# Last feed-forward product: the odd whole block and the half block by Strassen's seven products, with their sums made in the gate and up stage

## The chip, the cores and the metric

The kernel runs on one core of one Trainium2 chip. The metric is the device time of that core in microseconds (us). The kernel before takes 1022.51 us, the median of 3 runs (1022.26 to 1022.66).

## What is computed

```python
g = sigmoid((x * gate_w).sum(-1))                     # one gate for each token
h_re, h_im = x @ dft_hid_re.T, x @ dft_hid_im.T
a = dft_seq_re @ h_re - dft_seq_im @ h_im             # FNet mixing, real part
b = (gelu(x @ w_gate) * (x @ w_up)) @ w_down          # feed-forward with a gated GELU
out = g * a + (1 - g) * b
```

There are S = 2048 tokens, D = 640 features and F = 1728 hidden features, all fp32. In blocks of 128, F is 13 whole blocks and a half block of 64. "The last feed-forward product" is the one by w_down.

## The kernel before

**Parts and tiles.** An fp32 product is made of three matmuls of fp32r parts (`mm3`, L97 to L101): high by high (L99), high by low (L100), low by high (L101). The high part of an operand is a copy on ACT (`high`, L80), the low part a subtraction on DVE (`low`, L83). Everything lives transposed, features on the 128 partitions and tokens along the free dimension in tiles of T = 512. The tokens are two halves `tp` of two tiles each. Raw data, parts and sums share 46 slots of 4 KB a partition (`slot`); single 128x512 tiles come from a second pool of 14 (`mtile`); the eight PSUM banks of 128x512 are shared too (`bank`). A tile taken from a pool waits until the last reader of the tile that was in it is done.

**Strassen.** Most products go by Strassen's method in its form with seven products and shared sums. The four blocks of the left operand are two blocks of input features by two blocks of output features, those of the right operand two blocks of features by the two tiles of a token half. Weights have the blocks A11, A12, A21, A22 and the sums S1 = A21 + A22, S2 = S1 - A11, S3 = A11 - A21, S4 = A12 - S2. Activations have B11 to B22 and the sums T1 = B12 - B11, T2 = B22 - T1, T3 = B22 - B12, T4, as they are called here up to sign. For five output blocks of 128 features, two pairs go by Strassen and the fifth (`e5`, L) by plain products.

**Order of the work.** Five stages follow one another on PE: (1) the first hidden block and the half block (`first_products`, `first_out`), which go to DRAM as `h0[tp]`: entries 0 and 1 are the whole block for the two token tiles, entries 2 and 3 the half block, stacked twice so that it fills 128 partitions; (2) the gate and up stage, hidden blocks f = 1 to 12; (3) the last feed-forward product; (4) the sequence DFT (`cseq`); (5) the hidden DFT and the mixing of the two branches.

*The gate and up stage* (loop at L1094) runs in an order fixed by hand for PE, ACT, DVE and POOL (`in_order`, L1093): each engine works its instructions off in the order in which they were traced. `gate_up` (L485) makes the products of one block for one token half and the gated GELU; from block 3 on, odd blocks come with products across the two halves (`together`, `together_up`). Its sums of activations are, among others, L535, L539, L546, L556 and L563. Finished blocks go from POOL's queue to DRAM (`keep`, L388: `hA`, and the sums `hT`). What is made ready for later blocks is a list of pieces, `fills`, each with a cost: `fill` (L1070) takes pieces from the front while their summed cost is behind 1.25 times the share of PE's work already issued. Among the pieces are the sums and the parts of the next block's weights (`make_w`: sums at L269 to L288, parts by `split`), last sums of the block before (`todo`), the sums of w_down's pair k (`sum_wd`, L590, loads and stores on SP) and the sums of x across the halves (`sums_across`, loads at L1030 on SP; the one called `xv` has its sums at L1034). Blocks also load kept sums (`load_across`: L1065, on POOL, tiles `xq` and `xu`) and, at step 5, the weights of the block after next (on SP).

*The last product* is a list of 28 turns (`kseq`, L716 to L719). For each token half tp they are (b = 0; k = 0 to 5), (0, leftover), (1, 0), (1, leftover), (1; 1 to 5): with b = 0 the four products that need no activation sums, with b = 1 the three others. k is a pair of hidden blocks; the "leftover" (k = NK = 6) is the odd whole block 0 and the half block. The loop (L1171) traces for turn i, in this order: `load_k(i + 3)` (L722, on SP), `split_k(i + 2)` (L771, the parts on ACT and DVE), `late()` (products with the gate and stores of results that are due, L836 and L837), now and then other work (`load_xn` of an x block for stage 4 at the turns in `XN_AT`, L26; the reductions of x for the gate), and `step_k(i)` (L828): the matmuls and, at the end of a group, the copies out of the banks. ACT and DVE run in traced order.

`products` (L812) is what a pair costs: with b = 0, X, Z and V take two `mm3` per bank pair and L takes four, 30 matmuls in all; with b = 1, X, Q, R and Y take 24. The leftover is not by Strassen in the kernel before: `left` (L848) takes an `mm3` for the whole block and, for the half block, two "narrow" matmuls. The half block's 64 input features leave half of the 128 rows free, and these rows carry the low part of the weights (`mx`), so that two matmuls do what otherwise takes three. With b = 0 it goes into V, Z and L (30 matmuls), with b = 1 into R and Y (20); `split_k` makes A11 - A21 and the like by two subtractions at L782. The leftover turn with b = 1 (turn 8, and 22 for the second half) takes the operands of the one with b = 0 (turn 6, and 20) over as they are.

Of the kernel before, what the change touches and what calls it, by code (L numbers as in the profile page):

```python
# [9 lines left out]
F32 = mybir.dt.float32  # L10
F32R = mybir.dt.float32r
AF = mybir.ActivationFunctionType
ALU = mybir.AluOpType

P = 128
S, D, F = 2048, 640, 1728
T = 512
# [5 lines left out]
NF = F // P  # L23
FR = F - NF * P
NK = (NF - 1) // 2
XN_AT = [1, 5, 18, 24]  # L26
GM_AT = [2, 17]
EORD = [0, 2, 1, 3, 4]
PAIRED = 3
# [6 lines left out]
def kernel(  # L36
# [33 lines left out]
    def slot(dt, shape, name):  # L70
        return pool.tile(shape, dt, tag="s4", name=name, bufs=46)

    def mtile(dt, name):
        return pool.tile([P, T], dt, tag="m", name=name, bufs=14)
# [4 lines left out]
    def high(hi, raw):  # L79
        nc.scalar.activation(hi, raw, AF.Copy)  # L80
# [4 lines left out]
    def split(hi, lo, raw):  # L85
        high(hi, raw)
        low(hi, lo, raw)
# [38 lines left out]
    wsu, wneg = ([dram.tile([P, 8, P], F32, tag=f"{n}{p}", name=f"{n}{p}") for p in range(ND)] for n in ("wsu", "wneg"))  # L126
    uA, uT = ([[dram.tile([P, 4, T], F32, tag=f"u{n}{j}{p}", name=f"u{n}{j}{p}") for p in range(ND)] for j in range(2)] for n in "AT")
    grd, gmd = ([dram.tile([1, 2 * T], F32, tag=f"{n}{p}", name=f"{n}{p}") for p in range(2)] for n in ("grd", "gmd"))
    wsd = [dram.tile([P, 8, P], F32, tag=f"wsd{k}", name=f"wsd{k}") for k in range(NK)]
    t4d = [dram.tile([P, 2, T], F32, tag=f"t4{p}", name=f"t4{p}") for p in range(2)]  # L130
    acc4 = dram.tile([P, 2, T], F32, tag="acc4", name="acc4")
# [7 lines left out]
    def at(hilo, i):  # L139
        h, l = hilo  # L140
        return h[:, i], l[:, i]
# [448 lines left out]
    def sum_wd(k):  # L590
# [11 lines left out]

        return [(0, load), (84, do), (84, do)]

    def sum_wu(p):


        r = [mtile(F32, f"ur{p}{k}").rearrange("p (b c) -> p b c", c=P) for k in range(2)]
        a21 = wsmall(F32, f"ua{p}")
        for k in range(2):  # L610
            nc.sync.dma_start(r[k], wu[p, :, 4 * k : 4 * k + 4])
        nc.sync.dma_start(a21, wu[p, :, 8:])
        yield
        if p > 1:
            for k, a, b in ((0, 0, 2), (0, 2, 4), (1, 0, 1), (1, 1, 4)):
                if p < 4 or (k, a) not in ((0, 0), (1, 0)):
                    v = r[k][:, a:b]
                    nc.scalar.activation(v, v, AF.Copy, scale=-1.0)
            if p < 4:
                nc.scalar.activation(a21, a21, AF.Copy, scale=-1.0)  # L620
            for k in range(2):
                nc.gpsimd.dma_start(wneg[p][:, 4 * k : 4 * k + 4], r[k])
            yield
        for _, do in sums_left(nc.gpsimd, r[0][:, 0:2], r[0][:, 2:4], r[1][:, 2:4], a21, wsu[p]):
            do()
        yield
# [95 lines left out]
    def load_k(i):  # L722


        tp, b, k = kseq[i]
        n = f"{tp}{b}{k}"
        if k == NK and b:
            return
        r = slot(F32, [P, 8, P], f"kw{n}")
        if k == NK:  # L730
            m = slot(F32, [P, 8, P], f"km{n}")
            nc.sync.dma_start(r[:, :5], wd0)
            for q in range(2):
                nc.sync.dma_start(m[q * FR : (q + 1) * FR, :5], wdr)
            r, src = (r, m), h0[tp]
        elif b:
            nc.sync.dma_start(r[:, 0:2], wd[k, :, 6:8])
            nc.sync.dma_start(r[:, 2:8], wsd[k][:, 0:6])
            src = hT[tp][k]
        else:  # L740
            nc.sync.dma_start(r[:, 0:6], wd[k, :, 0:6])
            nc.sync.dma_start(r[:, 6:8], wsd[k][:, 6:8])
            src = hA[tp][k]
        raw = []
        for q in range(2):
            raw.append(pair(F32, f"kr{n}{q}"))
            nc.sync.dma_start(raw[q], src[:, 2 * q : 2 * q + 2])
        kraw[i] = r, raw
# [22 lines left out]
    def split_k(i):  # L771
        tp, b, k = kseq[i]
        n = f"{tp}{b}{k}"
        if k == NK and b:
            ktile[i] = ktile[("left", tp)]
            return
        r, raw = kraw.pop(i)
        W = {}
        if k == NK:
            r, m = r  # L780
            for v in (r, m):
                tt(v[:, 5:7], v[:, 0:2], v[:, 2:4], op=ALU.subtract)  # L782
            h, l = slot(F32R, [P, 8, P], f"kh{n}"), slot(F32R, [P, 8, P], f"kl{n}")
            split(h[:, :7], l[:, :7], r[:, :7])
            c, a = slot(F32R, [P, 8, P], f"kc{n}"), slot(F32R, [P, 8, P], f"ka{n}")
            high(c[:, :7], m[:, :7])
            high(a[:FR, :7], m[:FR, :7])
            low(c[FR:, :7], a[FR:, :7], m[FR:, :7])
            W = [at((h, l), q) for q in range(7)], [a[:, q] for q in range(7)]
        else:  # L790
            h, l = slot(F32R, [P, 8, P], f"kh{n}"), slot(F32R, [P, 8, P], f"kl{n}")
            split(h, l, r)
            names = ("A22", "S1", "S2", "S3") if b else ("A11", "A12", "e5", "S4")
            W = {name: (at((h, l), 2 * q), at((h, l), 2 * q + 1)) for q, name in enumerate(names)}
        B = []
        for q in range(2):
            v = hl(f"kb{n}{q}")
            split(*v, raw[q])
            B += [at(v, 0), at(v, 1)]
        ktile[i] = W, B  # L800
        if k == NK:
            ktile["left", tp] = W, B

    kb = {"alone": False}
    after = []
# [22 lines left out]
    def step_k(i):  # L828
# [14 lines left out]
                kb[name] = [bank(f"k{name}{n}{q}") for q in range(2)]  # L843
        X, Z, V, L, Q, R, Y = (kb.get(name) for name in "XZVLQRY")
        if k == NK:
            (f0, mx), first = W, False

            def left(ps, w, t):  # L848
                mm3(ps, f0[w], B[t], False, False)
                for v in B[2 + t]:  # L850
                    nc.tensor.matmul(ps, mx[w], v, start=False, stop=True, skip_group_check=True)

            if b:
                for q in range(2):
                    left(R[q], 2 + q, 1)
                for q in range(2):
                    left(Y[q], 2 + q, 0)
            else:
                for q in range(2):
                    left(V[q], q, 0)  # L860
                for q in range(2):
                    left(Z[q], 5 + q, 1)
                for t in range(2):
                    left(L[t], 4, t)
        else:
            products(kb, b, W, B, fst)
        if not lst:
# [225 lines left out]
    with in_order(PE, ACT, DVE, POOL):  # L1093
        for f in range(1, NF):  # L1094
# [24 lines left out]
            if kind == 1 and f > PAIRED:  # L1119
                (_, first), z1, (_, second), z2 = load_z(2)  # L1120
                first()
                k = len(fills) // 2
                more = list(fills)
                fills.clear()
                fills.extend([*more[:k], z1, (0, second), *more[k:], z2, *work])
            elif f in ZE_AT:
                (_, first), z1 = load_z(1)
                first()
                fills.insert(5, z1)
            if f == NF - 1:  # L1130
                load_k(0)
                fills.extend(split_pieces(0))
                gates(0)
                nc.scalar.activation(table, table, AF.Gelu_apprx_tanh)
# [447 lines left out]
```

## Time and profile before

| quantity | value |
|---|---|
| time, median of 3 runs | 1022.51 us (1022.26 to 1022.66) |
| span of the profiled execution | 1020.7 us |
| matmuls (PE) | 1016.5 us busy, 4491 instructions |
| weight loads (PEld) | 841.3 us, 4491 |
| VectorE (DVE) | 811.4 us, 1143 |
| ScalarE (ACT) | 481.3 us, 631 |
| GpSimd (POOL) | 166.9 us, 295 |
| DMA | 259.19 MB, 254 GB/s on average |

The span runs from the first to the last instruction of one profiled execution; the timed runs hold 1.8 us more around it. DVE is VectorE, ACT ScalarE, SP and POOL the engines that issue DMAs. Rows of the timeline give start, duration, engine, line, operation, and "output<-inputs" by the program's names, in which numbers of buffers are left out in some views; a bracket gives the idle time ahead and what ended it. Rows of the DMA list give output<-input, queue, operation, count, KB of each and the median from issue to landing. Rows of stretches give, for A:B us, the length, then the busy time (and count) of PE, PEld, DVE, ACT and POOL, the granted clock of TensorE, the busy share of the DMA engines and GB/s.

### The profile page before, as it was taken

What the parts mean: (1) busy time and instruction counts of PE and PEld (TensorE: products, weight loads), DVE (VectorE), ACT (ScalarE), POOL (GpSimd) and SP (SyncE); (2) the same over time, 40 slices, a digit from 0 to 9 for tenths busy, and PEclk for the clock granted to TensorE, in tenths of its full rate; (3) what the DMA queues carried; (4) which work ended last, traced back from release to release, by engine and by line L of the source; (5) the groups of instructions that cost most, each with busy time, mean ns of one, the idle gap of its engine ahead of it and who ended that gap; (6) DMA issues with size and microseconds to landing.
All of it is one profiled execution on the core that took longest, in us unless ns stands there. A gap on an engine that the chain in (4) does not pass through costs nothing.

```text
span 1020.7 us, 13172 instructions
## 1 busy us (share of the span) xinstructions
PE 1016.5 (100%) x4491; PEld 841.3 (82%) x4491; DVE 811.4 (79%) x1143; ACT 481.3 (47%) x631; POOL 166.9 (16%) x295
## 2 busy tenths in 40 slices
PE   9999999999999999999999999999999999999998
PEld 7888888888888888888888888888888888888887
DVE  6976878777677979886898975898588859797796
ACT  5544534353535566465455343444344444454440
POOL 0122242323231200100011022102210200021112
PEclk9999999999999999999999999999999999999999
DMA  7445587968698988968766788658866867987856
GB/s 270 168 152 212 181 270 251 295 216 292 201 309 297 406 319 305 358 229 303 269 233 190 249 265 310 215 193 293 302 207 209 298 248 274 324 318 221 264 150 95
DMA packets 92628, 259.19 MB, mean 254 GB/s; under 512 B 12112, under 2 KB 26576, under 8 KB 92560
## 3 DMA queue, kind: packets, MB, share of 16 engines
q1 hardware_dynamic: 66640, 176.98, 50.6%
q0 software_dynamic: 25776, 81.30, 24.6%
q8 instruction: 35, 0.57, 0.2%
q14 instruction: 33, 0.27, 0.1%
q10 hardware_dynamic: 144, 0.07, 0.0%
HBM read 186.19 MB, written 68.17 MB: 249 GB/s over the span
## 4 chain that ended last, share of the span: by engine, by line
PE 100%; DVE 0%; issue 0%
PE pX L101 7%; PE pX L99 7%; PE pX L100 7%; PE pZ L101 5%; PE pZ L99 5%; PE pZ L100 5%; PE pL L101 3%; PE pL L99 3%; PE pL L100 3%; PE pV L101 2%; PE pV L99 2%; PE pV L100 2%; PE pY L101 1%; PE pR L101 1%; PE pQ L101 1%; PE pY L100 1%
## 5 line engine op out<-in xcount | busy, mean ns | idle before, releaser
L80 ACT ACTIVATE ch<-csa 128x1024 fp32r<-128x1024 f32 x32 | 34.0, 1063 | 89.7 <-DVE csa L703 66.9
L83 DVE TENSOR_TENSOR cl<-cra,ch 128x1024 fp32r<-128x1024 f32 x32 | 39.1, 1223 | 21.7 <-ACT ch L80 21.5
L80 ACT ACTIVATE ch<-cra 128x1024 fp32r<-128x1024 f32 x32 | 33.9, 1059 | 46.2 <-PE pL L100 16.9
L83 DVE TENSOR_TENSOR cl<-crb,ch 128x1024 fp32r<-128x1024 f32 x32 | 39.1, 1222 | 17.3 <-ACT ch L80 17.3
L100 PE MATMUL pL<-cl,xah 128*128 128x512 f32 x128 | 49.8, 389 | 0.0
L101 PE MATMUL pL<-ch,xal 128*128 128x512 f32 x128 | 49.8, 389 | 0.0
L99 PE MATMUL pL<-ch,xah 128*128 128x512 f32 x128 | 49.3, 389 | 0.0
L388 POOL DMA_DIRECT2D hA<-s x48 | 26.1, 544 | 133.6 <-DVE s L546 113.9
L80 ACT ACTIVATE ch<-crb 128x1024 fp32r<-128x1024 f32 x32 | 33.8, 1055 | 27.5 <-DVE cl L83 11.0
L83 DVE TENSOR_TENSOR cl<-csb,ch 128x1024 fp32r<-128x1024 f32 x32 | 39.2, 1224 | 4.4 <-ACT ch L80 2.3
L83 DVE TENSOR_TENSOR cl<-csa,ch 128x1024 fp32r<-128x1024 f32 x32 | 39.1, 1223 | 3.8 <-PE pR L100 1.7
L83 DVE TENSOR_TENSOR kl<-kw,kh 128x1024 fp32r<-128x1024 f32 (+1 forms) x26 | 31.5, 1213 | 11.1 <-ACT kh L80 11.0
L80 ACT ACTIVATE ch<-csb 128x1024 fp32r<-128x1024 f32 x32 | 34.0, 1062 | 12.3 <-PE pR L101 4.5
L540 ACT ACTIVATE s<-s 128x512 f32<-128x512 f32 x24 | 15.2, 634 | 47.0 <-DVE s L539 47.0
L80 ACT ACTIVATE kh<-kw 128x1024 fp32r<-128x1024 f32 (+1 forms) x26 | 27.1, 1042 | 11.2 <-PE kY L101 3.3
L1243 POOL DMA_DIRECT2D uA<-c x8 | 4.3, 541 | 169.6 <-DVE c L1331 169.3
L837 POOL DMA_DIRECT2D out<-ks x12 | 6.5, 542 | 155.1 <-DVE ks L836 154.5
L145 ACT ACTIVATE s<-pX 128x512 f32<-128x512 f32 x40 | 23.3, 595 | 14.7 <-PE pX L101 14.4
L388 POOL DMA_DIRECT2D hT<-s x48 | 26.0, 541 | 24.2 <-DVE s L563 9.3
L535 DVE TENSOR_TENSOR s<-s,pX 128x512 f32<-128x512 f32 x24 | 16.4, 685 | 15.4 <-PE pX L101 15.4
L100 PEld LDWEIGHTS pL<-cl,xah 128*128 128x128 f32 x128 | 24.0, 188 | 5.0
L101 PEld LDWEIGHTS pL<-ch,xal 128*128 128x128 f32 x128 | 24.0, 188 | 5.0
(3602 smaller groups left out, 3462.0 us busy)
## 6 DMA issues: line engine op xcount, KB each, us to landing
cra<-in_ct SPq DMA_DIRECT2D x64, 512.0 KB, 4.0
crb<-in_ct SPq DMA_DIRECT2D x64, 512.0 KB, 4.9
hA<-s POOLq DMA_DIRECT2D x48, 256.0 KB, 3.8
hT<-s POOLq DMA_DIRECT2D x48, 256.0 KB, 5.5
kr<-hA SPq DMA_DIRECT2D x24, 512.0 KB, 7.4
kr<-hT SPq DMA_DIRECT2D x24, 512.0 KB, 6.9
ux<-uA SPq DMA_DIRECT2D x24, 512.0 KB, 6.3
ux<-uT SPq DMA_DIRECT2D x16, 512.0 KB, 6.3
```

The costliest lines, as they stand in the source:

```text
L80: nc.scalar.activation(hi, raw, AF.Copy)
L83: nc.vector.tensor_tensor(lo, raw, hi.bitcast(F32), op=ALU.subtract)
L99: nc.tensor.matmul(ps, lh, rh, start=first, stop=False, skip_group_check=True)
L100: nc.tensor.matmul(ps, lh, rl, start=False, stop=False, skip_group_check=True)
L101: nc.tensor.matmul(ps, ll, rh, start=False, stop=last, skip_group_check=True)
L145: nc.scalar.activation(m, src, AF.Copy)
L388: nc.gpsimd.dma_start(to[:, i], src)
L535: tt(s5, s5, X, op=ALU.add)
L540: nc.scalar.activation(s2, s2, AF.Gelu_apprx_tanh)
L837: nc.gpsimd.dma_start(acc4[:, t] if tp and e == 4 else out[2 * tp + t, e], src)
L1243: nc.gpsimd.dma_start(to[:, i], src)
```

## The change

The leftover is taken as one more pair of hidden blocks for Strassen: the whole block 0 and the half block. Where the half block stands for A21, A22, B21 or B22, the missing 64 rows count as zero.

- New sums are made in the gate and up stage and kept in DRAM: `wsl` for the weights, `hL[tp]` for the activations. `LEFT_AT` says in which block: 2 (`sum_h0` for tp 0), 4 (`sum_left`, the weights), 6 (`sum_h0_narrow` for tp 0), 8 and 10 (the same two for tp 1). They have their loads and stores on SP and stand in the middle of the block's `fills`.
- The leftover turn with b = 0 now goes into X as well (A11), and takes narrow matmuls alone for V (A12) and Z (S4); L stays as it was. The turn with b = 1 goes by S1, S3 and S2 into R, Q and X, and by narrow matmuls into Y. It loads activations of its own from `hL`, and takes over the weights alone.
- The subtractions in `split_k` go.
- The second x block for stage 4 is traced at turn 7, no longer at turn 5 (`XN_AT`).

```diff
--- before.py
+++ after.py
@@ -23,7 +23,7 @@
 NF = F // P
 FR = F - NF * P
 NK = (NF - 1) // 2
-XN_AT = [1, 5, 18, 24]
+XN_AT = [1, 7, 18, 24]
 GM_AT = [2, 17]
 EORD = [0, 2, 1, 3, 4]
 PAIRED = 3
@@ -126,6 +126,8 @@
     wsu, wneg = ([dram.tile([P, 8, P], F32, tag=f"{n}{p}", name=f"{n}{p}") for p in range(ND)] for n in ("wsu", "wneg"))
     uA, uT = ([[dram.tile([P, 4, T], F32, tag=f"u{n}{j}{p}", name=f"u{n}{j}{p}") for p in range(ND)] for j in range(2)] for n in "AT")
     grd, gmd = ([dram.tile([1, 2 * T], F32, tag=f"{n}{p}", name=f"{n}{p}") for p in range(2)] for n in ("grd", "gmd"))
+    wsl = dram.tile([P, 8, P], F32, tag="wsl", name="wsl")
+    hL = [dram.tile([P, 4, T], F32, tag=f"hL{p}", name=f"hL{p}") for p in range(2)]
     wsd = [dram.tile([P, 8, P], F32, tag=f"wsd{k}", name=f"wsd{k}") for k in range(NK)]
     t4d = [dram.tile([P, 2, T], F32, tag=f"t4{p}", name=f"t4{p}") for p in range(2)]
     acc4 = dram.tile([P, 2, T], F32, tag="acc4", name="acc4")
@@ -602,6 +604,78 @@
 
         return [(0, load), (84, do), (84, do)]
 
+    def chunks(name):
+        return mtile(F32, name).rearrange("p (b c) -> p b c", c=P)
+    def sum_left():
+        w, m, d = chunks("lw"), chunks("lm"), chunks("ld")
+        nc.sync.dma_start(w, wd0[:, :4])
+        for q in range(2):
+            rows = slice(q * FR, (q + 1) * FR)
+            nc.sync.dma_start(m[rows], wdr[:, :4])
+            nc.sync.dma_start(d[rows], wd0[:FR, :4])
+        a11, a21, a22 = w[:, 0:2], w[:, 2:4], m[:, 2:4]
+        own = {}
+        def first():
+            s = own["s"] = chunks("ls")
+            tt(s[:, 0:2], a21, a11, op=ALU.subtract)
+            tt(a21[:FR], a21[:FR], a22[:FR], op=ALU.add)
+            tt(m[:, 0:2], m[:, 0:2], a22, op=ALU.subtract)
+        def second():
+            s = own["s"]
+            tt(a11, a11, a21, op=ALU.subtract)
+            tt(d[:, 0:2], d[:, 0:2], d[:, 2:4], op=ALU.subtract)
+            tt(s[:, 2:4], m[:, 0:2], d[:, 0:2], op=ALU.add)
+            nc.sync.dma_start(wsl[:, 0:4], w)
+            nc.sync.dma_start(wsl[:, 4:8], s)
+        return [(100, first), (100, second)]
+    def sum_h0(tp):
+        f1, f2, b22 = (mtile(F32, f"lf{tp}{k}") for k in range(3))
+        for v, k in ((f1, 0), (f2, 1), (b22, 3)):
+            nc.sync.dma_start(v, h0[tp][:, k])
+        def first():
+            tt(f1, f2, f1, op=ALU.subtract)
+            for k in (0, 2):
+                rows = slice(FR if k else 0, P)
+                nc.sync.dma_start(hL[tp][rows, k], f1[rows])
+            tt(f2[:FR], f2[:FR], b22[:FR], op=ALU.subtract)
+            nc.sync.dma_start(hL[tp][:, 3], f2)
+            tt(b22[:FR], f1[:FR], b22[:FR], op=ALU.subtract)
+            nc.sync.dma_start(hL[tp][:FR, 2], b22[:FR])
+        return [(183, first)]
+    def sum_h0_narrow(tp):
+        d1, d2, b21, b22 = (mtile(F32, f"lg{tp}{k}") for k in range(4))
+        for v, k in ((d1, 0), (d2, 1)):
+            for q in range(2):
+                nc.sync.dma_start(v[q * FR : (q + 1) * FR], h0[tp][:FR, k])
+        for v, k in ((b21, 2), (b22, 3)):
+            nc.sync.dma_start(v, h0[tp][:, k])
+        def first():
+            tt(d2, d2, d1, op=ALU.subtract)
+            tt(b21, b21, b22, op=ALU.subtract)
+        def second():
+            tt(b21, b21, d2, op=ALU.add)
+            nc.sync.dma_start(hL[tp][:, 1], b21)
+        return [(122, first), (61, second)]
+    LEFT_AT = {2: partial(sum_h0, 0), 4: sum_left, 6: partial(sum_h0_narrow, 0), 8: partial(sum_h0, 1), 10: partial(sum_h0_narrow, 1)}
     def sum_wu(p):
 
 
@@ -724,14 +798,19 @@
 
         tp, b, k = kseq[i]
         n = f"{tp}{b}{k}"
+        r = None
+        if not (k == NK and b):
+            r = slot(F32, [P, 8, P], f"kw{n}")
         if k == NK and b:
-            return
-        r = slot(F32, [P, 8, P], f"kw{n}")
-        if k == NK:
+            src = hL[tp]
+        elif k == NK:
             m = slot(F32, [P, 8, P], f"km{n}")
-            nc.sync.dma_start(r[:, :5], wd0)
+            nc.sync.dma_start(r[:, 0:2], wd0[:, 0:2])
+            nc.sync.dma_start(r[:, 2:8], wsl[:, 0:6])
             for q in range(2):
                 nc.sync.dma_start(m[q * FR : (q + 1) * FR, :5], wdr)
+            nc.sync.dma_start(m[:, 5:7], wsl[:, 6:8])
+            nc.sync.dma_start(m[:, 7], wd0[:, 4])
             r, src = (r, m), h0[tp]
         elif b:
             nc.sync.dma_start(r[:, 0:2], wd[k, :, 6:8])
@@ -771,22 +850,22 @@
     def split_k(i):
         tp, b, k = kseq[i]
         n = f"{tp}{b}{k}"
+        r, raw = kraw.pop(i)
         if k == NK and b:
-            ktile[i] = ktile[("left", tp)]
-            return
-        r, raw = kraw.pop(i)
-        W = {}
-        if k == NK:
+            W = ktile.pop(("left", tp))
+        elif k == NK:
             r, m = r
-            for v in (r, m):
-                tt(v[:, 5:7], v[:, 0:2], v[:, 2:4], op=ALU.subtract)
-            h, l = slot(F32R, [P, 8, P], f"kh{n}"), slot(F32R, [P, 8, P], f"kl{n}")
-            split(h[:, :7], l[:, :7], r[:, :7])
             c, a = slot(F32R, [P, 8, P], f"kc{n}"), slot(F32R, [P, 8, P], f"ka{n}")
-            high(c[:, :7], m[:, :7])
+            high(c, m)
             high(a[:FR, :7], m[:FR, :7])
             low(c[FR:, :7], a[FR:, :7], m[FR:, :7])
-            W = [at((h, l), q) for q in range(7)], [a[:, q] for q in range(7)]
+            low(c[:, 7], a[:, 7], m[:, 7])
+            h, l = slot(F32R, [P, 8, P], f"kh{n}"), slot(F32R, [P, 8, P], f"kl{n}")
+            split(h, l, r)
+            W = {name: (at((h, l), 2 * q), at((h, l), 2 * q + 1)) for q, name in enumerate(("A11", "S2", "S1", "S3"))}
+            mx = {"A12": (a[:, 0], a[:, 1]), "A22": (a[:, 2], a[:, 3]), "e5": a[:, 4], "S4": (a[:, 5], a[:, 6])}
+            W = W, (c[:, 7], a[:, 7]), mx
+            ktile["left", tp] = W
         else:
             h, l = slot(F32R, [P, 8, P], f"kh{n}"), slot(F32R, [P, 8, P], f"kl{n}")
             split(h, l, r)
@@ -798,8 +877,6 @@
             split(*v, raw[q])
             B += [at(v, 0), at(v, 1)]
         ktile[i] = W, B
-        if k == NK:
-            ktile["left", tp] = W, B
 
     kb = {"alone": False}
     after = []
@@ -843,25 +920,28 @@
                 kb[name] = [bank(f"k{name}{n}{q}") for q in range(2)]
         X, Z, V, L, Q, R, Y = (kb.get(name) for name in "XZVLQRY")
         if k == NK:
-            (f0, mx), first = W, False
-
-            def left(ps, w, t):
-                mm3(ps, f0[w], B[t], False, False)
-                for v in B[2 + t]:
-                    nc.tensor.matmul(ps, mx[w], v, start=False, stop=True, skip_group_check=True)
+            W, e5, mx = W
+            def narrow(ps, w, v):
+                for part in v:
+                    nc.tensor.matmul(ps, w, part, start=False, stop=True, skip_group_check=True)
 
             if b:
+                for ps, w, t in ((R, "S1", 0), (Q, "S3", 3), (X, "S2", 2)):
+                    for q in range(2):
+                        mm3(ps[q], W[w][q], B[t], False, True)
                 for q in range(2):
-                    left(R[q], 2 + q, 1)
-                for q in range(2):
-                    left(Y[q], 2 + q, 0)
+                    narrow(Y[q], mx["A22"][q], B[1])
             else:
                 for q in range(2):
-                    left(V[q], q, 0)
+                    mm3(X[q], W["A11"][q], B[0], False, True)
                 for q in range(2):
-                    left(Z[q], 5 + q, 1)
+                    narrow(V[q], mx["A12"][q], B[2])
+                for q in range(2):
+                    narrow(Z[q], mx["S4"][q], B[3])
                 for t in range(2):
-                    left(L[t], 4, t)
+                    mm3(L[t], e5, B[t], False, False)
+                    narrow(L[t], mx["e5"], B[2 + t])
         else:
             products(kb, b, W, B, fst)
         if not lst:
@@ -1127,6 +1207,11 @@
                 (_, first), z1 = load_z(1)
                 first()
                 fills.insert(5, z1)
+            if f in LEFT_AT:
+                more = LEFT_AT[f]()
+                k = len(fills) // 2
+                rest = [fills.pop() for _ in range(len(fills) - k)]
+                fills.extend([*more, *reversed(rest)])
             if f == NF - 1:
                 load_k(0)
                 fills.extend(split_pieces(0))
```

## The prediction

> **What bounds the kernel now.** I read the page first, then what TensorE (PE) waited for, then stretches of the span, then the two engines that feed PE around the changed turns.
>
> ```profile
> span 1020.7 us, 13172 instructions
> PE 1016.5 (100%) x4491; PEld 841.3 (82%) x4491; DVE 811.4 (79%) x1143; ACT 481.3 (47%) x631; POOL 166.9 (16%) x295
> PE 100%; DVE 0%; issue 0%
> PE idle L935 <- PEq L1570: 0.8, 1, 0.8
> 340.00:360.00 20.00, 20.00 (x90) 16.57 (x89) 19.43 (x25) 9.96 (x13) 3.25 (x6) 1.00 1.03 400
> 380.00:400.00 20.00, 20.00 (x90) 16.57 (x89) 17.22 (x20) 13.95 (x16) 2.16 (x4) 1.00 0.88 310
> ```
>
> PE is busy for 1016.5 of 1020.7 us, the chain that ended last is PE throughout, and the list of its waits has a single row, 0.8 us ahead of the first matmul. In the last product (third number of the two stretches) PE is busy 20.00 of 20.00 us at a granted clock of 1.00, while DVE is busy 19.43 and 17.22. So time falls only with the number of matmuls, and rises only where a feeder comes too late. The medians of the timed runs (1022.51 us) lie 1.8 us above this span; I carry that 1.8 us over unchanged.
>
> **The matmuls.** The last product's turns show what a matmul costs:
>
> ```profile
> 374.20 0.62 PE L99 MATMUL kV<-kb0060h,kh 128*128 128x512 f32 x2
> 381.00 0.39 PE L99 MATMUL kX<-kb0100h,kh 128*128 128x512 f32 x1
> 386.44 0.39 PE L99 MATMUL kR<-kb0060h,kh 128*128 128x512 f32 x1
> 390.98 0.39 PE L99 MATMUL kX<-kb0110h,kh 128*128 128x512 f32 x1
> 396.42 0.61 PE L99 MATMUL kX<-kb0120h,kh 128*128 128x512 f32 x2
> 398.46 0.39 PE L100 MATMUL kQ<-kb0121l,kh 128*128 128x512 f32 x1
> ```
>
> The leftover turn 6 begins at 374.20, turn 7 at 381.00, leftover turn 8 at 386.44, turn 9 at 390.98, turn 10 at 396.42. Turn 7 has 24 matmuls in 5.44 us: 0.2267 us each. Turn 6 has 30 (three kinds of bank, two each, 3 + 2 matmuls): 6.80 us. Turn 8 has 20: 4.54 us. All are 128x512.
>
> In the changed kernel turn 6 has 6 (X) + 4 (V) + 4 (Z) + 10 (L) = 24 matmuls, 6 fewer, and turn 8 has 6 + 6 + 6 + 4 = 22, 2 more. Net 4 fewer for each half of the tokens, 8 in all: 4491 becomes 4483. 8 x 0.2267 = **1.81 us off**. That is the whole gain: the sums that Strassen needs are paid elsewhere. The Trainium skill (TensorE: Matmul & The Clock Gate, Back-to-back issue gap) gives about 131 ns for a sustained 512-column matmul; by it the gain would be 1.05 us. The trace's spacing is 227 ns, and the trace decides.
>
> **The new sums in the gate and up stage.** Twenty more DVE operations in blocks 2, 4, 6, 8 and 10: three of 128x512 (two with 64 rows) in 2, 6, 8 and 10, six of 128x256 in 4. In the built order they follow the first sums of the next block's weights (L284) and stand ahead of L269 (in block 2, of the low part L83). Rows of the same shapes, and what comes behind them:
>
> ```profile
> 125.97 0.69 DVE L556 TENSOR_TENSOR s<-s,s 128x512 f32<-128x512 f32 x1
> 126.58 0.69 DVE L546 TENSOR_TENSOR s<-s,s 128x512 f32<-128x512 f32 x1
> 132.10 0.42 DVE L274 TENSOR_TENSOR ws5r<-ws5r,wa5r 128x256 f32<-128x256 f32 x1
> DVE wd L83 <- ACT wd L80: 12.1, 5, 3.3
> 83.04 1.23 DVE L83 TENSOR_TENSOR wa3l<-wa3r,wa3h 128x1024 fp32r<-128x1024 f32 x1 [2.68 <-ACT wa3h L80]
> 229.01 0.29 DVE L288 TENSOR_TENSOR wb<-wa9r 128x128 f32<-128x128 f32 x1
> 231.85 0.29 DVE L83 TENSOR_TENSOR wd<-wb,wd 128x128 fp32r<-128x128 f32 x1 [2.56 <-ACT wd L80]
> 233.20 0.68 DVE L535 TENSOR_TENSOR s<-s,pX 128x512 f32<-128x512 f32 x1
> 236.68 0.39 PE L99 MATMUL pX<-x05h,wa 128*128 128x512 f32 x1
> ```
>
> One 128x512 sum follows the other after 0.61 us (125.97 to 126.58): three are 1.8 us. Six of 0.34 to 0.42 us are 2.0 to 2.5 us. Right behind the insertion DVE stands idle already: in block 2 for 2.68 us, in the later ones 2.4 us on average (12.1 us in 5 waits, up to 3.3), waiting for ACT's high part. That idle time takes 1.8 us whole, and of 2.0 to 2.5 us nearly all. I also cost it without the cover: block 8's L535 reads X at 233.20 to 233.88 and PE writes X again at 236.68, so 2.8 us of lead; a full shift of 1.8 or 2.5 us leaves 0.3 to 1.0 us. Cost on PE: **0**.
>
> POOL's queue holds one thing behind these sums: the load of the kept sums (L1065) takes a buffer that L288 reads last.
>
> ```profile
> 275.95 0.28 DVE L288 TENSOR_TENSOR wb<-wa11r 128x128 f32<-128x128 f32 x1
> 278.58 0.56 POOL L1065 DMA_DIRECT2D xq<-xp  x1 [0.41 <-issue]
> xq<-xp POOLq DMA_DIRECT2D x12, 512.0 KB, 5.0
> 286.40 0.39 PE L99 MATMUL pZ11t<-xq,wq11h 128*128 128x512 f32 x1
> 276.00:278.00 2.00, 2.00 (x10) 1.67 (x9) 0.23 (x2) 1.60 (x4) 0.70 (x1) 1.00 0.69 135
> kr<-hA SPq DMA_DIRECT2D x24, 512.0 KB, 7.4
> ```
>
> In block 10 L288 ends at 276.23; plus 1.8 it ends at 278.0, just ahead of the issue at 278.58. The load lands after 5.0 us by the median, at 283.6, 2.8 us ahead of PE. New is SP's store of 256 KB beside it; at the 135 GB/s of that stretch it takes 1.9 us if nothing overlaps. Bounds: 0 from the median, (278.58 + 7.4 + 1.9) - 286.40 = 1.5 us of wait from the slower row of 7.4. I take 0, nearer to the row of the same load.
>
> SP's queue: 41 more transfers, about 10 MB beside 259.19 MB on the page. In block 2 the four stores wait for DVE's sums, and the loads of the t4 sums stand behind them.
>
> ```profile
> 72.63 5.46 SPq L1030 DMA_DIRECT2D xv<-t  x4
> 80.08 0.29 DVE L284 TENSOR_TENSOR wq3r<-wa3r,wq3r 128x128 f32<-128x128 f32 x1
> 96.32 0.69 DVE L1034 TENSOR_TENSOR xvt<-xv,xv 128x512 f32<-128x512 f32 x1
> xr<-in_xt SPq DMA_DIRECT2D x11, 256.0 KB, 4.8
> ```
>
> The sums end at about 80.3 + 1.8 = 82.1; two of the four loads also wait for buffers that those stores read, so they go out by about 85 and land, at 4.8 us like other 256 KB loads, at about 90. DVE wants them at 96.32: 6 us to spare. Cost 0.
>
> **The last product's own feeders.** Turn 8 now has operands of its own: two more pairs of high and low part (ACT and DVE), four in all; the two subtractions at L782 go. And the x block moves from turn 5 to turn 7, into the densest place, between the operands of turns 9 and 10.
>
> ```profile
> 375.69 1.07 ACT L145 ACTIVATE ks<-kX 128x512 f32<-128x512 f32 x2
> 381.20 0.60 ACT L145 ACTIVATE ksl<-kL 128x512 f32<-128x512 f32 x1 [0.31 <-PE kL L851]
> 381.70 1.05 ACT L80 ACTIVATE kh<-kw 128x1024 fp32r<-128x1024 f32 x1
> 385.06 1.22 DVE L83 TENSOR_TENSOR kb0111l<-kr,kb0111h 128x1024 fp32r<-128x1024 f32 x1
> 386.19 1.29 DVE L836 TENSOR_TENSOR ks<-ks,gm 128x512 f32<-128x512 f32 x2
> 388.60 1.22 DVE L83 TENSOR_TENSOR kl<-kw,kh 128x1024 fp32r<-128x1024 f32 x1
> 389.74 1.22 DVE L83 TENSOR_TENSOR kb0120l<-kr,kb0120h 128x1024 fp32r<-128x1024 f32 x1
> 372.08 0.96 DVE L83 TENSOR_TENSOR xal<-xn,xah 128x768 fp32r<-128x768 f32 x1
> 375.82 0.96 DVE L83 TENSOR_TENSOR xbl<-xs,xbh 128x768 fp32r<-128x768 f32 x1 [0.28 <-ACT xbh L80]
> ```
>
> ACT's copies of L (381.20) wait for turn 6's end, and the split of turn 9 stands behind them. Turn 6 is 1.36 us shorter, so all this moves to 1.36 us earlier: turn 9's last low part ends at 386.28 - 1.36 = 384.9. The four products with the gate take 388.60 - 386.19 = 2.4 us, to 387.3. Then the x block: 372.08 to 376.78, 4.7 us, to 392.0; turn 10's high parts stand behind it on ACT. Three low parts at 1.14 us apart (388.60, 389.74) end at about 395.5. PE in the changed kernel comes to turn 10 at 374.20 + 5.44 + 5.44 + 22 x 0.2267 + 5.44 = 395.5, and reads the last of these low parts 2.0 us later (398.46 against 396.42), at 397.5. So **2 us of lead** remain where some 6 were (kb0121l, the part after 389.74, ended at 392.1). The later turns gain: three low parts, 3.4 us of DVE, to 5.44 us of PE. Cost 0, and from 2 us of further delay it costs PE one for one.
>
> A new wait: turn 6 now writes X, so ACT copies X inside it. X is done after about ten matmuls, at 376.6; two copies of 0.53 us end at 377.7; turn 7 writes X at 379.6. Lead 1.9 us, cost 0. For the second half of the tokens the same holds, with its x blocks where they were.
>
> **Sum.** 1020.7 - 1.81 = 1018.9 us of span; 1022.51 - 1.81 = **1020.7 us**, 0.18% less. A measurement of this kernel can tell about 0.2% (2.05 us) from no change, so this lies within it.
>
> **The rivals.**
>
> *Short waits* (0.10). The two thin places, 1.5 us at most in block 11 and a turn 10 whose x block comes late, each give back a part: 1020.7 to about 1022.8. For it: both are thinned by this change. Against it: each row taken alone leaves cover.
>
> *Slower* (0.14): the t4 loads behind the stores in SP's queue. DVE runs in a fixed order; when L1034 waits for its load, everything behind it waits, the operations that free PE's banks in block 3 among them. It decides once the loads land over 6 us later than worked out, at 96.3. To come out 2.05 us slower, PE must lose 3.9 us, so a landing at about 101: price about 1025 us. For it: these loads went out at 72.63 and now wait for DVE. Against it: the longest median of the rows above is 7.4 us, and 85 + 7.4 is 92.4. By the Trainium skill (TensorE: Matmul & The Clock Gate, The HAM clock gate) about 3.4 us without work halves PE's clock for the next such window, an estimate of 1.7 us more, 1027. No row here shows it: the granted clock is 1.00 and the longest wait 0.8 us.
>
> *It does not do what it says*: the count would stay near 4491 and the time at 1022.5. The built order has 8 fewer matmuls, so I give this nothing of its own.
>
> **How the numbers follow.** The case without new waits has 0.76, around 1020.7; the three runs before span 0.4 us, so of it I give 0.12 to below 1020.46 (over 0.2% faster) and 0.64 to within. Short waits are within too: 0.74 in all. Slower has 0.14. The range goes from 0.4 us under the sum, 1020.3, to the upper end of the short waits, 1022.8; left out are the slower rival and a little of the lowest edge.
>
> **What would show it.** Right: 4483 matmuls, a span near 1018.9, a single PE wait of 0.8 us, turn 6 of 5.44 and turn 8 of 4.99 us, in blocks 4 to 10 a shorter DVE wait for wd, xv loads issued at 82 to 85. Wrong: rows of PE waits at pZ11t (xq), at the first low parts of turn 10, or at block 3's banks; matmuls of the new turns with another spacing than 0.2267 us.

## The result, and the profile after

The changed kernel takes 1025.47 us, the median of 10 runs (1022.09 to 1029.92), beside 1022.7 us (1022.26 to 1023.21) for the kernel before in as many runs. The ratio is 1.0029, interval 1.0016 to 1.0042: **slower by 0.29%**, where 1020.7 us and "within 0.2%" was forecast. Its runs lie 7.8 us apart, those of the kernel before 1.0 us. The profiled execution is the shortest of the ten (1022.09 us), so it shows where PE waits, but not the waits of the median run. Ratios here and below go by all runs of a kernel, so a few long runs can lift one above 1 where the median lies below the kernel before.

Three lines of the page after: span, busy times and the chain that ended last.

```profile
span 1020.3 us, 13287 instructions
PE 1015.7 (100%) x4483; PEld 839.3 (82%) x4483; DVE 824.0 (81%) x1163; ACT 486.0 (48%) x635; POOL 166.9 (16%) x295
PE 88%; issue 8%; POOL 2%; DVE 1%; DMA 1%; POOLq 0%; DVEq 0%
```

The 8 matmuls are gone (4491 to 4483). But the chain, 100% PE before, now goes through POOL and transfers, with 8% of issue. What PE waited for (line, what ended it, sum, times, longest):

```profile
PE idle L1015 <- PEq L1655: 0.8, 1, 0.8
PE pH5t L99 <- DMA xq<-xp: 0.3, 1, 0.3
```

The second row is new. At that place in the timeline:

```profile
145.98 0.39 PE L101 MATMUL pV5t<-x05h,wa5l 128*128 128x512 f32 x1
146.72 0.50 PE L99 MATMUL pH5t<-xq,wq5h 128*128 128x512 f32 x1 [0.35 <-DMA xq<-xp]
147.06 0.39 PE L100 MATMUL pH5t<-xq,wq5h 128*128 128x512 f32 x1
```

From start to start this is 0.74 and 0.34 us in place of 0.23 each: 0.62 us lost, more than the row of waits says, since a matmul counts as busy beyond the start of the next one. The way to look for small waits here is the distance of the starts. By it this trace loses 1.1 us in all: 0.8 in block 5, the rest in blocks 9 and 11. The span lies 1.4 us above the 1018.9 of the prediction.

The changed turns themselves are as they were worked out:

```profile
375.56 0.62 PE L99 MATMUL kX<-kb0060h,kh 128*128 128x512 f32 x2
381.00 0.39 PE L99 MATMUL kX<-kb0100h,kh 128*128 128x512 f32 x1
386.44 0.39 PE L99 MATMUL kR<-kb0160h,kh 128*128 128x512 f32 x1
391.43 0.39 PE L99 MATMUL kX<-kb0110h,kh 128*128 128x512 f32 x1
```

Turn 6 takes 5.44 us (6.80 before), turn 8 takes 4.99 (4.54).

Where the loss begins is seen on two queues in block 4. POOL before, the low part of wq by an accumulating transfer (L95) and the three loads of xq:

```profile
134.26 0.87 POOL L95 DMA_DIRECT2D wq5l<-wq5r  x1 [2.82 <-ACT wq5l L91]
135.66 0.56 POOL L1065 DMA_DIRECT2D xq<-xp  x1 [0.53 <-issue]
139.82 1.22 POOL L1065 DMA_DIRECT2D xq<-xp  x2 [3.60 <-DVE s L535]
```

POOL after:

```profile
134.39 0.87 POOL L95 DMA_DIRECT2D wq5l<-wq5r  x1 [2.82 <-DVE ws5r L271]
135.98 0.57 POOL L1145 DMA_DIRECT2D xq<-xp  x1 [0.72 <-DVE wb L290]
141.61 1.22 POOL L1145 DMA_DIRECT2D xq<-xp  x2 [5.07 <-DMA wq5l<-wq5r]
```

The second and third xq loads wait for the accumulating transfer. In the lists of transfers (last column: us from issue to landing) before and after:

```profile
wq5l<-wq5r POOLq DMA_DIRECT2D x1, 448.0 KB, 5.2
```

```profile
wq5l<-wq5r POOLq DMA_DIRECT2D x1, 448.0 KB, 6.8
```

SP before, in the same stretch:

```profile
118.36 0.43 SPq L216 DMA_DIRECT2D wb<-in_wf  x1
119.22 0.33 SPq L597 DMA_DIRECT2D da<-in_wd  x1
119.61 0.41 SPq L216 DMA_DIRECT2D wb<-in_wf  x1
```

SP after:

```profile
133.13 0.33 SPq L633 DMA_DIRECT2D wsl<-lw  x1
133.93 0.33 SPq L634 DMA_DIRECT2D wsl<-ls  x1
134.31 0.46 SPq L218 DMA_DIRECT2D wb<-in_wf  x1
134.82 0.59 SPq L599 DMA_DIRECT2D da<-in_wd  x1
135.46 0.47 SPq L218 DMA_DIRECT2D wb<-in_wf  x1
```

The stores of the new sums stand at the head of SP's queue and wait for DVE. Three loads of 128 KB, which had gone out at 118 to 120, stand behind them and now go out at 134 to 136, together with the stores, just when POOL's transfers run. In blocks 6, 8 and 10 these loads move by 15 to 19 us (in block 10 from 261.62 to 278.10).

### The profile page after: what moved, and what is told of

The parts are those of the page before. It is cut to its first block, busy times and chain, and to the rows that moved or that the text cites. A ratio compares the mean times of both kernels' runs of the same rounds, so it can differ in the third digit from the quotient of the medians.

```text
span 1020.3 us, 13287 instructions
## 1 busy us (share of the span) xinstructions
PE 1015.7 (100%) x4483; PEld 839.3 (82%) x4483; DVE 824.0 (81%) x1163; ACT 486.0 (48%) x635; POOL 166.9 (16%) x295
## 4 chain that ended last, share of the span: by engine, by line
PE 88%; issue 8%; POOL 2%; DVE 1%; DMA 1%; POOLq 0%; DVEq 0%
PE pX L100 5%; PE pX L99 5%; PE pX L101 5%; PE pZ L100 4%; PE pZ L99 4%; PE pZ L101 4%; PE pL L99 3%; PE pL L100 3%; PE pL L101 3%; PE pY L99 1%; PE pQ L99 1%; PE pR L99 1%; PE pV L99 1%; PE pV L100 1%; PE pR L101 1%
## 5 line engine op out<-in xcount | busy, mean ns | idle before, releaser
L83 DVE TENSOR_TENSOR kl<-kw,kh 128x1024 fp32r<-128x1024 f32 x26 | 31.7, 1220 | 6.5 <-ACT kh L80 6.5
L80 ACT ACTIVATE kh<-kw 128x1024 fp32r<-128x1024 f32 x26 | 27.2, 1048 | 2.1 <-DMA kw<-wsd 2.1
L99 PEld LDWEIGHTS pL<-ch,xah 128*128 128x128 f32 x128 | 24.0, 188 | 5.0
```

Of the source, the lines that this page charges most:

```text
L83: nc.vector.tensor_tensor(lo, raw, hi.bitcast(F32), op=ALU.subtract)
L99: nc.tensor.matmul(ps, lh, rh, start=first, stop=False, skip_group_check=True)
```

## The experiments

Each was run beside the kernel before (medians 1022.7 to 1022.9 us). Theory A: the transfers of the new sums slow POOL's loads; A1: by the stores' own bytes; A2: by the loads that they hold up. Theory B: DVE's time for the sums delays them. Theory C: the turns of the last product come late. e2, e3, e4 and e6 leave the sums or their stores out, whole or in part, so their results are not those of the program and only their times count.

### First set: which part

**e1, the changed kernel again.** 

> The changed kernel once more, so that its spread and a second trace stand beside the runs below. If its waits at the xq and xu tiles are what costs: about 1025.5 us with single runs between 1022 and 1030, and PE waits in blocks 5, 7, 9 or 11 whose sum is the span's excess over 1018.9 us. If the last product's turns cost: PE waits between 370 and 470 us.

Measured: 1027.07 us (1022.33 to 1032.96), ratio 1.0043 (1.0024 to 1.0061). The profiled execution (1023.42 us) is again one of the short ones. PE's waits are in the gate and up stage, the longest at the xq tile of block 5; none is in the last product:

```profile
PE pH5t L99 <- DMA xq<-xp: 1.0, 2, 0.8
```

By the distance of the starts it loses 1.5 us in block 5, 0.4 in block 7, 0.3 in block 9 and 0.1 in block 11, which is 2.3 of the 2.7 us that its span (1021.6) lies above 1018.9. All four blocks lose. What the runs of 1027 to 1033 us lose, and where, no trace shows.

**e2, the turns alone.** `if f in LEFT_AT` and the stores go; two of the loads (the edit is longer):

```diff
-            src = hL[tp]
+            src = h0[tp]
...
-            nc.sync.dma_start(r[:, 2:8], wsl[:, 0:6])
+            nc.sync.dma_start(r[:, 2:8], wd[0, :, 0:6])
```

> Only the new leftover turns and the x block at turn 7; the sums in the gate and up stage are left out with their loads and stores, and the leftover turns load other data of the same size in their place. Theory A (transfers of the new sums slow POOL's loads) and theory B (the DVE time of the new sums delays them): 1022.7 - 1.8 = 1020.9 us, a spread of some 0.9 us like the kernel before, no PE wait but the first. Theory C (the turns themselves come late): 1023 to 1026 us, waits in the last product.

Measured: 1020.86 us (1020.51 to 1022.16), 0.9981 (0.9972 to 0.9989). C falls, and the 1.8 us of the sum are there: 1022.77 - 1020.86 = 1.9. All of the loss lies in the making of the sums.

**e3, sums without stores.** The `dma_start` into `hL` and `wsl` go, the loads of the turns as in e2. 

> The new sums are made on DVE where they are, with their loads, but not stored; the leftover turns load other data of the same size. Theory A: about 1021 us, the xq loads land as in the kernel before plus at most 0.5 us. Theory B: 1024 to 1026 us, the xq loads of blocks 5, 7, 9 and 11 land 2 to 4 us later than before, as in the changed kernel.

Measured: 1021.42 us (1020.76 to 1022.95), 0.9986 (0.9977 to 0.9994). DVE's time and the loads of the sums cost 0.56 us against e2; the stores, by their bytes or by what stands behind them, cost the other 4.05 to 5.65 us (1025.47 and 1027.07 less 1021.42).

**e4, stores without the sums.** Each sum works on 8 columns, and five of the eighteen are left out; one line of the edit:

```diff
-            tt(f1, f2, f1, op=ALU.subtract)
+            tt(f1[:, :8], f2[:, :8], f1[:, :8], op=ALU.subtract)
```

> The loads and stores of the new sums stay whole, their DVE operations work on 8 columns in place of 256 or 512 (so the sums are not made). Theory A: 1024 to 1026 us. Theory B: about 1021 us, the xq loads as in the kernel before.

Measured: 1025.11 us (1023.12 to 1030.47), 1.0027 (1.0013 to 1.004). B falls: with hardly any of DVE's time the loss is as large as in the changed kernel's first ten runs (1.0029). The same transfer of wq's low part in e3 and in e4:

```profile
wq5l<-wq5r POOLq DMA_DIRECT2D x1, 448.0 KB, 5.0
```

```profile
wq5l<-wq5r POOLq DMA_DIRECT2D x1, 448.0 KB, 6.5
```

### Second set: bytes or order

**e5, the stores behind the held-up loads.** The stores are traced at the end of the block's list and ordered on SP behind the loads:

```diff
+        for ins in behind.pop(f, []):
+            tc.add_manual_dep(ins, last.name, dep, reason="behind")
```

(two lines of a longer edit)

> The changed kernel with the same sums and stores, but in blocks 4 to 10 SP's queue has the loads that the stores held up (wb, da) ahead of the stores, as in the kernel before. Theory A1 (the stores' own bytes beside POOL's loads cost): 1024 to 1026 us. Theory A2 (the stores wait for DVE at the head of SP's queue, and the 384 KB of loads behind them move into the time of POOL's loads): about 1021.4 us like the run without stores, wq's accumulating loads back to 5.2 us.

Measured: 1032.21 us (1028.73 to 1034.3), 1.0087: both theories missed, by the edit's own fault, in two places. Beside blocks 4 to 10 it moved block 2, where the stores now stood ahead of two of the xv loads at 93.5 to 97 us. On SP, DVE and PE of e5:

```profile
93.53 0.99 SPq L659 DMA_DIRECT2D hL<-lf  x2
...
97.15 4.25 SPq L1125 DMA_DIRECT2D xv<-t  x2
```

```profile
103.06 0.69 DVE L1129 TENSOR_TENSOR xvt<-xv,xv 128x512 f32<-128x512 f32 x1 [6.20 <-DMA hL<-lf]
```

```profile
107.16 0.80 PE L99 MATMUL pH3t<-xp,wq3h 128*128 128x512 f32 x1 [4.83 <-ACT s L147]
107.75 0.63 PE L100 MATMUL pH3t<-xp,wq3h 128*128 128x512 f32 x1
108.18 0.63 PE L101 MATMUL pH3t<-xp,wq3l 128*128 128x512 f32 x1
```

```profile
107.00:112.00 5.00, 4.84 (x11) 3.84 (x12) 3.99 (x7) 2.61 (x5) 1.57 (x3) 0.50 0.30 120
```

This is the prediction's slower rival, made by accident: DVE waits 6.2 us at the first sum of xv (the row names one of these stores as what ended it), PE 4.8 us behind it, and then the matmuls follow each other at 0.43 us, to 112.87, at a granted clock of 0.50.

The second place is block 10: there the two loads of `da` stayed behind the store, as in the changed kernel, and went out at 285.62, with wq's accumulating transfer at 286.04. PE then waits 3.0 us for xq, where the traces of the changed kernel have 0.8 at most. That this order is the cause there is argued; e9, which mends it, has no such wait.

```profile
285.25 0.32 SPq L683 DMA_DIRECT2D hL<-lg  x1
285.62 1.06 SPq L603 DMA_DIRECT2D da<-in_wd  x2
```

```profile
PE pH11t L99 <- DMA xq<-xp: 3.0, 1, 3.0
```

From 301 to 304, behind this wait, the granted clock is 0.50 again.

**e6, small stores.** `wsl[:, 0, 0:16]`, `hL[tp][:, 3, 0:16]` and so on. 

> Every store of the new sums is cut to 16 columns in place of 256 to 512 (the sums are not kept; the leftover turns load other data of the same size). The stores wait for DVE in SP's queue as before, so the loads behind them move as in the changed kernel, but the stores have hardly any bytes. Theory A1: about 1021.4 us. Theory A2: 1023 to 1026 us.

Measured: 1022.5 us (1021.46 to 1027.12), 1.0003 (0.9991 to 1.0015). Between the two: order alone costs about 1.1 us against e3 in the median. But three of the eleven runs took 1026 to 1027 us, and in the trace the transfer of wq's low part in block 4 takes as long as in the changed kernel, and PE waits at pH5t:

```profile
wq5l<-wq5r POOLq DMA_DIRECT2D x1, 448.0 KB, 6.8
```

```profile
PE pH5t L99 <- DMA xq<-xp: 0.7, 1, 0.7
```

**e7, the stores on ACT's queue** (`nc.scalar.dma_start`). 

> The changed kernel with the stores of the new sums issued from ACT's queue. SP's loads are no longer behind them, the bytes go at the same time. Theory A1: 1024 to 1026 us. Theory A2: about 1021.5 us, and with 1.8 us gained for the turns it would beat both kernels; if ACT comes late by its waits for DVE's sums, some more.

Measured: 1027.64 us (1027.03 to 1028.09), 1.0046 (1.0033 to 1.0059). SP's `da` goes out at 123.78 again, but ACT stands behind the stores' waits for DVE: PE waits for ACT's copies in blocks 4, 6 and 8, and 1.3 us for xq in block 11. It tells nothing between A1 and A2. That another issuing queue doesn't take transfers out of each other's way is what the Trainium skill says (DMA: Bandwidth & Descriptors, Issuing engines are not separate DMA queues): all share the same 16 DMA engines. This run doesn't show it, since ACT's own waits lie on top.

**e8, the sums at the end of the same blocks' lists** (`fills.extend(LEFT_AT[f]())`). 

> The changed kernel with the new sums at the end of the same blocks' lists in place of the middle: DVE makes them behind the next block's weight parts, SP's order has the held-up loads ahead of the stores, and the stores go some 7 us later. Theory A1: 1022 to 1024 us, since the stores then lie beside the last of the xq loads. Theory A2: about 1021 us. Theory B has nothing against it, since nothing of the weight parts is delayed: 1020.9 us.

Measured: 1023.39 us (1022.28 to 1033.21), 1.0018 (1.0 to 1.0035). Better than the changed kernel in the median; three of the twelve runs took 1026.7 to 1033.2, and the trace is one of these (1026.73). In block 8 the stores now go out at 235.9 to 237.9, just ahead of the next loads, those of xz (241.6); that they collide is argued from these times. DVE and PE of e8 in block 9:

```profile
253.78 0.82 DVE L730 CUSTOM_DVE_ANT_0 xz<-xz,gwb 128x640 f32<-128x640 f32 x1 [5.76 <-DMA xz<-in_xz]
...
254.53 0.68 DVE L440 TENSOR_TENSOR s<-s,pH9t 128x512 f32<-128x512 f32 x1
```

```profile
255.27 0.79 PE L99 MATMUL pH9t<-x121h,wq9h 128*128 128x512 f32 x1 [2.20 <-DVE s L440]
```

```profile
255.00:259.00 4.00, 3.73 (x10) 2.96 (x11) 3.89 (x10) 2.31 (x4) 0.39 (x1) 0.57 0.37 145
```

The time is the one that A1 gave, but the wait in the trace is not at xq. DVE works in its fixed order: it waits for xz, the sum that frees PE's bank stands behind, PE waits 2.2 us, and the clock is 0.57 in the 4 us after it.

### Third set: the clean test, and another place

**e9, e5 with both places mended.** Block 2 stays as in the changed kernel; blocks 4, 6, 8 and 10 have the loads ahead of the stores, `da` in block 10 too; every sum and every byte is as in the changed kernel. 

> As the run with the stores behind, but block 2 is left as in the changed kernel; only in blocks 4, 6, 8 and 10 do the held-up loads (wb, da) stand ahead of the stores. The stores' bytes are the same and go at nearly the same time. A1 alone: 1024 to 1026 us, like the changed kernel. A2 alone: 1021.4 us. Both with half each, as the small stores suggest: about 1023 us.

Measured: 1021.89 us (1021.16 to 1023.15), 0.9993 (0.9984 to 1.0002). SP and POOL of e9 in block 4:

```profile
122.22 0.58 SPq L225 DMA_DIRECT2D wb<-in_wf  x1
122.84 0.44 SPq L607 DMA_DIRECT2D da<-in_wd  x1
123.33 0.43 SPq L225 DMA_DIRECT2D wb<-in_wf  x1
133.12 0.33 SPq L644 DMA_DIRECT2D wsl<-lw  x1
```

```profile
140.43 1.22 POOL L1165 DMA_DIRECT2D xq<-xp  x2 [3.90 <-DMA wq5l<-wq5r]
```

```profile
wq5l<-wq5r POOLq DMA_DIRECT2D x1, 448.0 KB, 5.7
```

The stores go out when they went out in the changed kernel (133.1), and the xq loads 1.2 us earlier (140.43 against 141.61). Reordering a few loads on one queue takes back 3.6 to 5.2 us of the loss. So the order is needed for it, and A1 alone falls. Against e3 the bytes alone cost 0.47 us and the order alone (e6) 1.08 us in the median; both together cost 4.05 us, and 5.65 in e1. **Most of the loss is their meeting.** How the two add up in each block is not shown: in e6's trace the order alone is enough for the wait in block 5.

**e10, the sums in odd blocks**, between the reduction of xz and the next block's weights:

```diff
-fills.extend([*more[:k], z1, (0, second), *more[k:], z2, *work])
+fills.extend([*more[:k], z1, (0, second), *more[k:], z2, *LEFT_AT[f](), *work])
```

> The changed kernel with the sums of blocks 4 to 10 moved to the odd blocks 5, 7, 9 (activations) and 11 (weights), between the reduction and the next block's weight parts, so that DVE's work and the stores lie where POOL loads no xq and frees no wq. If the collision with the xq loads is the whole loss: 1020.9 us, better than both kernels, no PE wait at xq. If any stores in this stage cost as much: 1024 us or more, with waits at the xu tiles.

Measured: 1022.5 us (1021.22 to 1023.83), 0.9995 (0.9987 to 1.0004): most of the loss is gone, but it doesn't beat the kernel before clearly.

**e11, e10 with the second x block back at turn 5.** 

> As the run with the sums in the odd blocks, but with the second x block at turn 5 as in the kernel before. If moving the x block was not needed: the same time within 0.3 us. If turn 7 or 8 comes late by the four high and low parts that turn 8 now has: a PE wait of up to 2 us at turns 7 to 9.

Measured: 1022.19 us (1021.19 to 1028.98), 1.0006 (0.9993 to 1.002). No PE wait in the last product, and the median is that of e10 within 0.3 us: where the x block stands doesn't show there. Three of the twelve runs took 1025.4 to 1029.0, where e10 has none above 1023.83; why is open.

### Fourth set: the rest of about 1 us

By the distance of the starts, the traces of e2, e9, e10 and e11 each lose 0.3 to 1.0 us at one place in a middle block, at pH9t or pH11t, where DVE waited 2.8 to 4.6 us at the reduction of xz, as in e8.

**e12, e13, e14: both reductions of xz later on DVE** (`[*more[:k], (0, second), *more[k:], z1, *work, z2]`), on e9, on e10 and on the kernel before.

> As the run with the stores behind in blocks 4 to 10, and in the odd blocks from 5 on the two reductions of xz stand later on DVE: behind the sums that free PE's H bank. If the reductions' wait for their loads is what is left: 1021.0 us, spread under 1 us, no PE wait at pH9t or pH11t. If it is something else: 1021.9 us.

> As the run with the sums in the odd blocks, with the two reductions later on DVE in the same way. If the reductions' wait is what is left: 1021.0 us. If the stores in the odd blocks or something else cost: 1022.5 us.

> The kernel before, with the two reductions later on DVE in the same way and nothing else. It has no PE wait in its trace: the same 1022.5 us within 0.3, with fewer single runs above 1023.

Measured: 1030.4 us (1.0067, 1.0053 to 1.0081), 1040.64 (1.0179, 1.0165 to 1.0193) and 1025.78 (1.0031, 1.0021 to 1.0042), in 5, 4 and 7 runs. All missed. The wait is gone and others stand in its place, in e14 too. The longest of PE's waits in e14:

```profile
PE pV5u L99 <- ACT pV5u L458: 1.3, 1, 1.3
```

**e15, e16, e17: only the first reduction, behind the sum L440**, on e9, on the kernel before and on e10 (z1 two pieces later).

> As the run with the stores behind in blocks 4 to 10, and in blocks 5, 7, 9 and 11 the first reduction of xz stands on DVE behind L440, L445 and L446 in place of ahead of L440. If the reduction's wait for its load is the rest: 1021.0 us, without the PE wait at pH9t or pH11t. If not: 1021.9 us.

> The kernel before with the same move of the first reduction. No PE wait is to be had there: 1022.6 us within 0.3. If the move itself makes something late, as moving both did: above 1023.5 us.

> As the run with the sums in the odd blocks, with the first reduction behind L440. If the reduction's wait is its rest: 1021.0 us. If the stores in the odd blocks cost: 1022.5 us.

Measured: 1024.02 us (1.0008, 0.9999 to 1.0017), 1022.9 (1.0001, 0.9992 to 1.001) and 1025.53 (1.0031, 1.002 to 1.0042). e15 and e17 missed. Again the named wait goes, and PE's waits in e15, as in e17, are now at xu:

```profile
PE pH9u L99 <- DMA xu<-xv: 1.3, 1, 1.3
PE pH7u L99 <- DMA xu<-xv: 0.6, 1, 0.6
```

The sums that free the buffers of xu (`sums_left`, L589 in e15) stand behind the moved reduction. On the kernel before the same move costs nothing (e16).

**e18, fewer bytes**: the halves that repeat h0 or another sum aren't stored (`hL[tp][:FR, 3]` for `hL[tp][:, 3]`), on e9. 

> As the run with the stores behind in blocks 4 to 10 (1021.89 us), but the half of the activation sums that only repeats h0 or another sum is not stored, 512 KB in place of 768 KB in blocks 2 and 8; the leftover turn takes it from where it stands already, by two loads more. If the remaining 1 us is the stores' bytes: about 1021.5 us and clear of the kernel before. If it is the DVE time and the loads of the sums: 1021.9 us. If the two more loads make turn 8 late: above 1022.5 us with a PE wait at turn 8.

Measured: 1022.58 us (1021.07 to 1024.26), 0.9997 (0.9988 to 1.0006), above both sizes that were expected of the bytes: no gain that can be told from e9. The trace has no PE wait at turn 8, but one of 0.9 us at xu in block 9. So the remaining 1 us is not settled. The waits that are left in the traces lie in the odd blocks, and no version that keeps all the sums beats the kernel before clearly; e9, at 0.9993, comes nearest.

## Why the prediction was wrong, point by point

- **The matmuls: right.** 4483, turns of 5.44 and 4.99 us, and the turns alone give 1.9 us where 1.81 was worked out (e2). The interval of e2 (0.9972 to 0.9989) also shows that with eleven runs a gain of 0.19% can be told from none.
- **DVE's sums in idle time: nearly right.** DVE's wait for wd fell from 1.8 us to 1.0 on average over the whole run (before and after: sum, times, longest; the five waits of which the prediction spoke fell from 2.4 to 1.2), and e3 loses 0.56 us to DVE's time and the loads together. In block 2 the wait did not shrink (3.44 us beside 2.68), and PE has no wait there. The count was loose: twenty is the difference over the whole program, the sums listed for these blocks are eighteen. Of the transfers there are 45 more, not 41.

```profile
DVE wd L83 <- ACT wd L80: 12.9, 7, 3.3
DVE wd L83 <- ACT wd L80: 6.9, 7, 1.9
```

- **POOL's queue: this step failed**, the "I take 0" for the xq loads. "POOL's queue holds one thing behind these sums: the load of the kept sums takes a buffer that L288 reads last." That is the first of three xq loads. The second and third wait for wq's accumulating transfer, whose duration the step didn't look at; the row quoted there even shows an x1, and the list says x12 for four blocks. And beside the transfer it put only the bytes of the store (1.9 us). That the store waits for DVE in SP's queue, and what stands behind it there, was followed in block 2 and not in blocks 4 to 10. The runs show in its place: in each of the four blocks, loads move by 15 us and more onto POOL's transfers (SP rows above), wq5l takes 6.8 us in place of 5.2, and xq comes late; with the loads ahead of the stores wq5l takes 5.7 us and 3.6 to 5.2 us come back (e9). The term put at 0 measured 4.05 us in the median (1025.47 - 1021.42), beside the 0.56 us of DVE's time and the sums' loads.
- **Block 2: right.** The xv loads went out from 82.02 on and DVE used them at 96.45. The rival that hung on them has a real mechanism: in e5, where DVE came to this sum at 103.06, PE waited 4.8 us and then ran at half clock to 112.87.
- **The last product's feeders: right.** kb0121l ends at 395.57 + 1.22 = 396.79 in the changed kernel and PE reads it at 399.14: a lead of 2.35 us where 2 was forecast, and no wait.
- **The clock.** "No row here shows it": the runs do. The Trainium skill (TensorE: Matmul & The Clock Gate, The HAM clock gate) puts the half clock after an idle window of about 3.4 us; here a wait of 2.2 us was enough in e8, with some seven matmuls 0.43 us apart behind it, and the measurement decides. It doesn't always follow: in e12 a wait of 1.9 us (to 214.56) has a clock of 0.54 behind it (216.5 to 219), one of 1.8 us (to 164.69) a clock of 1.00 (165 to 169). So a wait of about 2 us can cost more than its length. The half clock doesn't make the long upper end of the changed kernel's times by itself. The mean granted clock of each run is on record: the longest has 0.998 (1029.92 us) and in e1 0.996 (1032.96), but the runs of 1027.45 and 1027.66, and in e1 those of 1031.0 and 1031.31 us, have 1.000. What those lose is waits, in places that no trace shows.
- **The short waits had 0.10 and ended at 1022.8.** The mechanism was named, at the right tile (the first of its three loads, where the other two come late), and mis-sized: 1.5 us in one block, where four blocks lose (e1), on the median some 4.6 us together (1025.47 - 1020.86, e2). Their chance rested on one profiled execution, in which the leads looked whole. The same kernel spans 1022 to 1033 us (e1), and wq5l takes 6.8 us in one of its traces and 7.2 in the other. That landings which change from run to run make this spread is argued, since only short runs were traced; if so, a lead of 2 to 3 us over a transfer of 5 us is not a cover but a chance, drawn again in each block.

## What to carry to other kernels

When a store that waits for a compute engine is put into a queue, list what stands behind it there, and ask into whose time those transfers move; its own bytes were the smaller part here (0.5 us alone). Where every lead is a few us, a change that frees an engine still has to pay for each transfer it adds, and mending one wait uncovers the next: price the whole set of leads (how long before its use does each load land, and by how much do loads vary) before trusting a sum of 0.2%. One profiled execution shows the places; the spread of the times shows whether they are thin.

## What the hardware showed beyond that

A PE wait of 2.2 us was followed by a granted clock of 0.57 over 4 us (e8), one of 4.8 us by 0.50 over 5 us (e5), with matmuls 0.43 us apart in place of 0.23; of two waits of 1.8 and 1.9 us in one execution (e12) only the second was. Two sets of transfers that cost 0.5 and 1.1 us alone cost 4 to 5.7 us together, in the medians.
